# Sums of the hidden-DFT weights kept in DRAM, and seven block products from the second group on

## The chip, the cores and the metric

The kernel runs on one core of one Trainium2 chip. The metric is the time of one execution on the device in microseconds; the time before is 2187.01 us, the median of three runs (2182.2 to 2187.72).

A core has five engines that run side by side and wait for one another through semaphores: PE (TensorE, matrix multiply; PEld is its weight load), DVE (VectorE), ACT (ScalarE), POOL (GpSimd) and SP (SyncE). In this kernel SP issues every DMA, in program order, from one queue. On-chip data lie in SBUF, matmul results in eight PSUM banks, the rest in DRAM.

## The reference

Four layers work on `x` of 2048 rows by 640 columns: attention, Fourier mixing, attention, Fourier mixing. The change concerns the second kind:

```python
a = jnp.einsum("bsd,ed->bse", x, dft_hid_re)
b = jnp.einsum("bsd,ed->bse", x, dft_hid_im)
y = jnp.einsum("ts,bse->bte", dft_seq_re, a) - jnp.einsum("ts,bse->bte", dft_seq_im, b)
x = x + y   # with the layer norm of x as input of a and b
```

Both Fourier layers use the same weights. They are layers 1 and 3 here (layers are counted from 0).

## The kernel before, in words

**Precision.** A float32 operand is cut into a high part (an ACT copy to float32r) and a low part (a subtraction on DVE or POOL), and each product is three matmuls: high by high, high by low, low by high. `split` (L224 to L233) and `cut_part` (L1534 to L1541) do this.

**A Fourier layer** turns the order of the reference round. First come the *sequence passes* (`seq`, L1384): four passes, one for each half of the rows `sb` and part (cosine, sine), each with three stages "a", "b" and "g" of eight units. They multiply the normalized input by the sequence weights `c` and leave the result `u`, transposed, in DRAM (`u_d`). The passes keep a hand-made pipeline: `load_to(n + 3)` issues the loads of `c`, `cut_to(n + 2)` cuts them into a ring of buffers about two units ahead of PE, `x_to` cuts the other operand, and `gather` (L1447) copies or adds up the accumulators at a stage's end. Its stores to `u_d` are put into a list, and `leave` issues them later. The first pass of layer 1 is mixed with the attention before it; that of layer 3 uses sums of `c` which layer 1 kept in DRAM.

Then comes the *column product*: `u` times the 640 x 640 hidden weights `wr`, `wi`. It runs over eight groups `g` of two row tiles (128 rows each). A group by `eight` (L1659) does all eight block products, as two halves of 320 columns for each row tile, with 30 matmuls each: 120 in all. A group by `seven` (L1686) uses a scheme of seven block products with 15 matmuls each, 105 in all, with sums of `u` blocks (`u_s1`, `u_s4`, and `differences` in place) and sums of weight blocks ("t1", "t3", "t4", "t2"). Its order is b11, t1, b21, t2, t3, b22, t4; after each product, adds on DVE and POOL take the bank into the row tiles. The two row tiles of group `g` are `raws[2g]` and `raws[2g + 1]`, each of 640 columns: `x22` is the right half of the second one, and `add(nc.vector, x22, v, x22)` follows t1.

Groups 3, 4, 5 of layer 1 and 3 to 7 of layer 3 are sevens (L1579). Groups 6 and 7 of layer 1 stay eights, with work for the next layer between them.

**The weights' sums.** `load_sums` (L1543 to L1554) loads the ten raw tiles `wr[k]`, `wi[k]` (k = 0 to 4, 128 x 640 each) at the start of the column product, and `make_sums(k)` (L1556 to L1570) makes the four block sums of one k with two adds on POOL, two on DVE, and two splits. They are called between the halves of groups 1 and 2, in both layers, and written to `big2`, `big3` and, for k = 4, two tiles "wt".

**What sets the order around the change.** At the start of the column product SP's queue holds, in this order: three `leave` stores of `u_d`, row tiles 0 and 1, `load_u(1, 1)`, four raw weight tiles, six more stores, `load_u(2, 0)`, row tile 2, six raw weight tiles. Then the group loop begins, with row tile 3 first. `kp1` has room for three `u` loads, the pool "x" for five row tiles. `big2` and `big3` hold the input of the sequence passes until stage "g" of the last pass has cut its last unit. While a seven runs, `coming(g + 1, ...)` makes and cuts the first two operands of the next group.

Of the kernel before, what the change touches and what calls it, by code (L numbers as in the profile page):

```python
# [60 lines left out]
def pairs(c):  # L61
    return [(c[2 * i], c[2 * i + 1]) for i in range(len(c) // 2)]


class Net:
    def __init__(self, nc, tc, ctx, a):
        self.nc, self.tc, self.a = nc, tc, a
        const = ctx.enter_context(tc.tile_pool(name="const", bufs=1))
        self.ln = ctx.enter_context(tc.tile_pool(name="ln", bufs=5))
        self.slots = ctx.enter_context(tc.tile_pool(name="slots", bufs=1))  # L70
        psum = ctx.enter_context(tc.tile_pool(name="psum", bufs=1, space=PSUM))
        self.work = ctx.enter_context(tc.tile_pool(name="work", bufs=2))
# [22 lines left out]
        self.cd = dram.tile([3, NB // 2, P, 512], F32, name="c_d")  # L95
        self.sums_kept = False
# [12 lines left out]
        self.seen = fixed("seen", 2, F32)  # L109
# [1084 lines left out]
    def take_fourier(self):  # L1194
        def halves(t):
            return t.rearrange("p (l c) -> p l c", l=2)

        w = [self.work.tile([P, 2 * D], F32, name="s3", tag="wc") for _ in range(2)]
        self.s3 = sum([cuts(t[:, :1024], 256) for t in w], [])
        self.raws = [t[:, :1024] for t in w + [self.pt[2], self.pt[0], self.pt[1]]]  # L1200
        p = [cuts(t, 512) for t in self.pt]
        self.t1 = p[3] + [self.vq[2]] + self.ou + [p[0][2], p[1][2]]
        half = NB // 2
        first = [("a1", j) for j in range(half)] + [("a2", j) for j in range(half - 1)]
        first += [("b7", 0), ("a2", half - 1), ("b7", 1), ("b5", 0), ("b5", 1)]
        first += [("b", j) for j in range(2, half)] + [("g", j) for j in range(half)]
        self.last_a2 = first.index(("a2", half - 1))
# [176 lines left out]
    def seq(self, n):  # L1384
# [54 lines left out]
        if last and not soon:  # L1439
            self.gather(sb, part, ph)  # L1440

    def leave(self, n=9):
        for f in self.leaving[:n]:
            f()
        del self.leaving[:n]
# [94 lines left out]
        self.nc.vector.tensor_tensor(out=l, in0=src, in1=h.bitcast(F32), op=OP.subtract)  # L1540
        self.made.append((cuts(hi, P), cuts(lo, P)))  # L1541

    def load_sums(self):  # L1543

        c = [self.work.tile([P, 2, 512], F32, name="wt", tag="c", bufs=3).rearrange("p l c -> p (l c)")[:, :D]
             for _ in range(3)]
        self.w_raw = [c[:2], [c[2], self.raw()]]
        for k in range(KC):
            if k == 2:
                yield  # L1550
                self.w_raw += [cuts(t, D) for t in cuts(self.take_qk("kp", 0, F32), 2 * D)]
            for n, t in zip(("wr", "wi"), self.w_raw[k]):
                self.nc.sync.dma_start(t, self.a[n][:, k, :])
        yield  # L1554

    def make_sums(self, k):  # L1556
        nc = self.nc
        if k == 0:
            self.w_sum = sum([pairs(cuts(self.take_big(2 + i), 2 * D)) for i in range(2)], [])
            self.w_sum.append([self.work.tile([P, 2, D], F32R, name="wt", tag="wc").rearrange("p l c -> p (l c)")  # L1560
                               for _ in range(2)])
        r, i = self.w_raw[k]
        (r1, r2), (i1, i2) = cuts(r, 320), cuts(i, 320)
        nc.gpsimd.tensor_tensor(out=r1, in0=r2, in1=r1, op=OP.subtract)
        nc.gpsimd.tensor_tensor(out=r2, in0=r2, in1=i2, op=OP.add)
        nc.vector.tensor_tensor(out=i2, in0=i2, in1=r1, op=OP.add)
        nc.vector.tensor_tensor(out=i1, in0=i2, in1=i1, op=OP.subtract)
        hi, lo = self.w_sum[k]
        for n, t in enumerate((r, i)):
            self.parts_of(hi[:, n * D:(n + 1) * D], lo[:, n * D:(n + 1) * D], t)  # L1570

    def parts_of(self, hi, lo, t):
        self.split(hi, lo, t)

    def fourier(self, xsrc, xdst, more):
        nc = self.nc
        wc = pairs(sum([cuts(t, D) for t in self.big[:2]], []) + cuts(self.qp[0][:, :4 * D], D))
        self.u_raw, self.n_upl = {}, 0
        sevens = range(3, 6 if more else NB // 2)  # L1579
        self.made = deque()  # L1580
        loads = []

# [19 lines left out]
        for n in range(self.un, total):  # L1602
            if n == total - NB:
                weights(range(8))
            if n == total - NB // 2:
                weights(range(8, 10))
                self.take_qk("kp", 1, F32)
            self.seq(n)
            step_w()
            if n >= total - 5 and n < total - 2:  # L1610
                self.load_u((n - total + 5) // 2, (n - total + 5) % 2)
# [27 lines left out]
        def coming(g, n):  # L1639
# [5 lines left out]
                return  # L1645
            a11, a21, a22 = [self.quarter(g, *pz) for pz in ((0, 0), (0, 1), (1, 1))]
            if n == 0:
                add(nc.gpsimd, self.u_s1, a21, a22)
                self.cut_part(a11)
            else:  # L1650
                self.cut_part(self.u_s1)
# [7 lines left out]
        def eight(g, z, sums):  # L1659
            t = 2 * g + z  # L1660
            for n in range(2):
                if z:
# [11 lines left out]
            for hf in range(2):  # L1674
# [4 lines left out]
                add(nc.vector, raws[t][:, cs], p, raws[t][:, cs])  # L1679
                if z and hf:  # L1680
                    differences(g + 1)
                for k in sums[hf]:
                    self.make_sums(k)
            store_x(t)

        def seven(g, halfway):  # L1686
# [5 lines left out]
            def weight(name, k):  # L1692
                if name[0] == "b":
                    k, c = k + KC * (name[1] == "2"), (int(name[2]) - 1) * 320
                    return [w[:, c:c + 320] for w in wc[k]]
                c = ("t1", "t3", "t4", "t2").index(name) * 320
                return [w[:, c:c + 320] for w in self.w_sum[k]]

            def product(p, name, start=True):
                hi, lo = self.made.popleft()  # L1700
# [6 lines left out]
            product(x, "b11")  # L1707
            nc.scalar.activation(p1, x, AF.Copy)
            self.cut_part(a12)
            add(nc.gpsimd, self.u_s4, a12, a11)  # L1710
            product(v, "t1")
            add(nc.vector, x22, v, x22)
            self.cut_part(a11)
# [25 lines left out]
        def before(t):  # L1739
            if not more:  # L1740
                return
            if t == 8:
                self.tmp = cuts(self.kp[0], D)
# [16 lines left out]
        def behind(t):  # L1760
            if more and t >= 12:
# [17 lines left out]
        next(sums)  # L1779
        self.u_sum = [self.slot_tile(n, 512, F32)[:, :320] for n in ("rr1", "rr2", "vq2")]  # L1780
        for g in range(NB // 2):
            load_x(2 * g + 1, 2 * g + 2)
# [4 lines left out]
                seven(g, lambda: before(2 * g + 1) if g < 5 else None)  # L1787
            else:
                for z in range(2):
                    at = 2 * g + z  # L1790
                    eight(g, z, {2: ((), (0,)), 3: ((1,), ()), 4: ((2,), (3,)), 5: ((4,), ())}.get(at, ((), ())))
                    behind(at)
        self.ready, self.hid, self.sums_kept = 8, False, True


# [70 lines left out]
```

## Time and profile before

| what | value |
|---|---|
| median of three runs | 2187.01 us (2182.2 to 2187.72) |
| the profiled execution's own time | 2187.93 us |
| its span, first to last instruction | 2186.2 us |
| granted clock of PE | 0.997 |
| PE / DVE / ACT / POOL busy | 2118.1 / 1603.7 / 1140.5 / 958.0 us |
| moved by DMA | 398.40 MB, mean 182 GB/s |
| later passes of layer 1 (second to fourth) | 678.1 to 973.2 us of the span |
| column product of layer 1 | from 973.17 us |
| column product of layer 3 | from 2051.20 us to the end |

How to read it: the profile is of one execution, and its times are microseconds from the span's start. In a group of instructions stand line, engine, operation, out<-in by the program's names, shapes and count, then busy time, the mean of one in ns, and the idle time before with what ended it. In a timeline stand start, length, engine, line, and in brackets the idle time before with what ended it. In a table of stretches stand start:end, length, the busy time and count of each engine in the order PE, PEld, DVE, ACT, POOL, the granted clock, the share of the 16 DMA engines, and GB/s. "SPq" rows are issues of DMAs, not the transfers.

### The profile page before, as it was taken

The numbers are of one execution on the slowest core, as the hardware profiler recorded it, in microseconds if no ns is written. First come the engines' busy times: TensorE is split into PE (matmuls) and PEld (weight loads), VectorE is DVE, ScalarE is ACT, GpSimd is POOL, SyncE is SP. The second block draws the span as 40 slices with busy tenths as digits, with TensorE's granted clock in tenths as the row PEclk, the third lists the DMA queues.
The fourth block names the chain that finished last, engine by engine and source line by source line (L and its number), as shares of the span: only waits on it lengthen the run. The fifth ranks groups of instructions, "written<-read, shape, count | busy, mean of one in ns | idle before, by whom it ended". The sixth has DMA issues, their size and how long they took to land.

```text
span 2186.2 us, 48927 instructions
## 1 busy us (share of the span) xinstructions
PE 2118.1 (97%) x17872; PEld 1783.2 (82%) x17872; DVE 1603.7 (73%) x3931; ACT 1140.5 (52%) x2125; POOL 958.0 (44%) x1562
## 2 busy tenths in 40 slices
PE   7999999988999999999999999999899999999999
PEld 7987777677878888889999877776778888888899
DVE  6358888886897868786661588888767968677676
ACT  3117777656554545452341177777565645445332
POOL 3037776765614222322430377767655033231324
PEclk9999999999999999999999999999999999999999
DMA  5546666785555354656645556567855454546653
GB/s 183 175 157 190 198 180 215 211 224 169 202 192 189 127 183 141 214 177 207 207 156 167 162 186 200 181 212 226 216 161 182 140 182 132 174 152 208 222 165 125
DMA packets 227089, 398.40 MB, mean 182 GB/s; under 512 B 39969, under 2 KB 86561, under 8 KB 226849
## 3 DMA queue, kind: packets, MB, share of 16 engines
q1 hardware_dynamic: 226848, 395.28, 57.3%
q8 instruction: 141, 2.31, 0.5%
q14 instruction: 100, 0.81, 0.1%
HBM read 273.94 MB, written 120.06 MB: 180 GB/s over the span
## 4 chain that ended last, share of the span: by engine, by line
PE 78%; DVE 7%; DMA 5%; ACT 4%; issue 3%; POOL 2%; SPq 1%; ACTq 0%; DVEq 0%; POOLq 0%
PE banks L1416 29%; PE banks L239 15%; PE banks L257 12%; PE banks L694 6%; PE banks L659 5%; PE banks L1704 5%; PE banks L631 5%; DMA qp<-qk_d 2%; DVE banks L636 1%; ACT pt L669 1%; DMA x_d<-x 1%; PE banks L341 1%; DMA kp<-qk_d 1%; ACT big L1039 1%; DVE qp L232 1%
## 5 line engine op out<-in xcount | busy, mean ns | idle before, releaser
L636 DVE CUSTOM_DVE_ANT_0 banks<-banks,mask 128x384 f32<-128x384 f32 (+2 forms) x1024 | 527.6, 557 | 123.0 <-PE banks L631 99.9
L669 ACT ACTIVATE pt<-banks 128x768 f32<-128x768 f32 (+2 forms) x512 | 393.8, 772 | 168.7 <-PE banks L659 55.2
L675 POOL TENSOR_SCALAR_AFFINE_SELECT pt<-pt 128x256 f32<-128x256 f32 x512 | 213.3, 417 | 213.8 <-ACT pt L669 192.0
L257 PE MATMUL banks<-big,wc 64*128 64x512 f32 x1920 | 271.1, 394 | 0.4 <-DVE pt L442 0.4
L659 PE MATMUL banks<-qp,kp 61*128 61x384 f32 (+2 forms) x1024 | 210.2, 381 | 22.8 <-DVE mc L636 17.4
L694 PE MATMUL banks<-pt,vq 128*32 128x128 f32 x5760 | 211.6, 278 | 3.5 <-ACT pt L669 3.4
L631 PE MATMUL banks<-kp,qp 60*128 60x384 f32 (+2 forms) x1024 | 205.5, 347 | 6.7 <-DVE mc L636 3.1
L257 PEld LDWEIGHTS banks<-big,wc 64*128 64x128 f32 x1920 | 186.8, 185 | 22.6 <-ACT x L544 1.5
L679 POOL TENSOR_SCALAR_AFFINE_SELECT pt<-pt 128x256 f32<-128x256 f32 x448 | 193.8, 433 | 0.0
L226 ACT ACTIVATE qp<-pt 128x512 fp32r<-128x512 f32 (+1 forms) x200 | 123.2, 625 | 128.1 <-DVE pt L1347 51.7
L232 DVE TENSOR_TENSOR qp<-pt,qp 128x512 fp32r<-128x512 f32 (+1 forms) x198 | 156.6, 798 | 42.1 <-ACT qp L226 40.5
L694 PEld LDWEIGHTS banks<-pt,vq 128*32 128x32 f32 x5760 | 142.4, 110 | 51.5 <-issue 35.3
L659 PEld LDWEIGHTS banks<-qp,kp 61*128 61x128 f32 x1024 | 108.0, 184 | 87.3 <-DVE mc L636 65.2
L1416 PE MATMUL banks<-qp,big 128*128 128x512 f32 x648 | 152.9, 390 | 0.0
L631 PEld LDWEIGHTS banks<-kp,qp 60*128 60x128 f32 x1024 | 123.6, 186 | 31.9 <-DVE mc L636 16.4
L1345 POOL TENSOR_TENSOR pt<-pt,pt 128x512 f32<-128x512 f32 x32 | 47.2, 1475 | 231.4 <-DMA pt<-c 173.4
L226 ACT ACTIVATE c<-pt 128x512 fp32r<-128x512 f32 x146 | 90.4, 625 | 111.1 <-POOL pt L1325 57.1
L636 DVE DVE_READ_ACCUMULATOR2_ANT mc<- 128x1 f32 x1024 | 145.0, 142 | 0.0
L1416 PEld LDWEIGHTS banks<-qp,big 128*128 128x128 f32 x648 | 120.8, 188 | 24.2
L232 DVE TENSOR_TENSOR c<-pt,c 128x512 fp32r<-128x512 f32 x144 | 113.8, 793 | 26.9 <-ACT c L226 24.4
L1416 PE MATMUL banks<-qp,xc 128*128 128x512 f32 x480 | 117.4, 391 | 4.3 <-DVE xc L232 2.8
L552 POOL CAST c<-x 128x512 fp32r<-128x512 f32 x64 | 38.9, 611 | 166.5 <-ACT x L544 162.3
(253 smaller groups left out, 4479.9 us busy)
## 6 DMA issues: line engine op xcount, KB each, us to landing
pt<-c SPq DMA_DIRECT2D x166, 512.0 KB
qk_d<-c SPq DMA_DIRECT2D x80, 512.0 KB
kp<-qk_d SPq DMA_DIRECT2D x384, 80.0 KB
qp<-qk_d SPq DMA_DIRECT2D x384, 80.0 KB
kp<-u_d SPq DMA_DIRECT2D x32, 640.0 KB
o_d<-ou SPq DMA_DIRECT2D x64, 256.0 KB
x_d<-x SPq DMA_DIRECT2D x48, 320.0 KB
v_d<-pt SPq DMA_DIRECT2D x16, 768.0 KB
```

The costliest lines, as they stand in the source:

```text
L226: nc.scalar.activation(hi, src, AF.Copy, scale=-1.0 if neg else 1.0)
L232: (eng or nc.vector).tensor_tensor(out=lo, in0=src, in1=hi.bitcast(F32), op=OP.subtract)
L239: self.nc.tensor.matmul(p, x, y, start=n == 0, stop=n == last)
L257: self.nc.tensor.matmul(ps[a], x[r], y[r], start=half + i == 0, stop=half == 1 and i == n - 1, skip_group_check=True)
L631: nc.tensor.matmul(p, qp[quad % 2][b:b + 60, z, qb * P:(qb + 1) * P], kp[quad % 2][b:b + 60, z, k0 * P:(qb + 1) * P], start=True, stop=True)
L636: nc.vector.tensor_tensor_reduce(out=p, in0=p, in1=self.mask[:, 384 - n * P:], scale=1.0, scalar=NEG, op0=OP.add, op1=OP.max, accum_out=mc ...
L659: nc.tensor.matmul(self.banks[:, banks[e], :n * P], kp[quad % 2][b:b + 61, z, kb * P:(kb + 1) * P], qp[quad % 2][b:b + 61, z, kb * P:(kb + ...
L669: nc.scalar.activation(pt[quad, kb][:, 2 * z:2 * z + 2, :n * P], self.banks[:, b0:b1 + 1, :n * P], AF.Exp, scale=SCALE)
L675: nc.gpsimd.affine_select(out=t[:, :, 0:P], in_=t[:, :, 0:P], pattern=[[0, 2], [1, P]], compare_op=OP.is_ge, fill=0.0, base=0, channel_mul ...
L679: nc.gpsimd.affine_select(out=t[:, :, 256:384], in_=t[:, :, 256:384], pattern=[[0, 2], [-1, P]], compare_op=OP.is_gt, fill=0.0, base=0, ch ...
L694: nc.tensor.matmul(self.banks[32 * h:32 * h + 32, bank, :P], vq[:, 96 * (kb % 4) + 21 * h:96 * (kb % 4) + 21 * h + 32], t[:, h, (qb - kb) ...
L1416: nc.tensor.matmul(self.banks[:, bk, :], p, b[q], start=start and m == 0, stop=stop and last and m == 2, skip_group_check=True)
```

## The change

The sums are made once, by a generator `weight_sums(k)`, in stages a and b of the second to fourth pass of layer 1. `weight_step` starts it at unit 1 of stage a (k = 0, 1 in the second pass, 2, 3 in the third, 4 in the fourth) and takes one step of it after each unit: load the two raw tiles; two units later two adds; two more adds; then a split and the stores of its high and low part, twice. All adds are on DVE. The parts are stored in a new DRAM tensor `w_d` of 5 x 4 tiles of 128 x 640.

In both layers `load_sums(k, n)` loads the high and low part of half n (n = 0: t1 and t3; n = 1: t4 and t2) of every k, twenty tiles in all, where ten raw tiles were loaded. The half n = 0 of k = 0 to 3 goes to `big2`, ahead of the first three `leave` stores; n = 1 goes to `big3`, after row tile 2. The calls of `make_sums` go. Sevens begin with group 1. The adds into `u_s1` and `u_s4` go from POOL to DVE. The release of `kp0`, which held the raw tiles of k = 2 to 4, moves to row tile 8.

```diff
+    def weight_sums(self, k):
+        got = [self.raw() for _ in range(2)]
+        for n, t in zip(("wr", "wi"), got):
+            nc.sync.dma_start(t, self.a[n][:, k, :])
+        yield
+        yield
+        (r1, r2), (i1, i2) = [cuts(t, 320) for t in got]
...
+        add(r1, r2, r1, OP.subtract)
+        add(r2, r2, i2)
+        yield
+        add(i2, i2, r1)
+        add(i1, i2, i1, OP.subtract)
+        yield
+        for n, t in enumerate(got):
+            h = self.ln.tile([P, D], F32R, name="x", tag="x")
+            self.split(h, t.bitcast(F32R), t)
+            yield
+            for m, x in enumerate((h.bitcast(F32), t)):
+                nc.sync.dma_start(self.wd[k, 2 * n + m], x)
+        yield
+
+    def weight_step(self, n):
+        if self.sums_kept or n < self.first_len:
+            return
+        sb, part, ph, j = self.order[n]
+        if ph == "a" and j == 1:
+            p = 2 * sb + part - 1
+            self.making = (f for k in ((0, 1), (2, 3), (4,))[p] for f in self.weight_sums(k))
+        if ph != "g":
+            next(self.making, None)
+
+    def load_sums(self, k, n):
+        if k < KC - 1:
+            big = self.big[2 + n]
+            places = [big[:, (2 * k + m) * D:(2 * k + m + 1) * D] for m in range(2)]
+        else:
+            places = cuts(self.work.tile([P, 2 * D], F32R, name="wt", tag="wc"), D)
+        for m, t in enumerate(places):
+            self.nc.sync.dma_start(t.bitcast(F32), self.wd[k, 2 * n + m])
+        self.w_sum[k, n] = places
...
-        sevens = range(3, 6 if more else NB // 2)
+        sevens = range(1, 6 if more else NB // 2)
...
             self.seq(n)
+            self.weight_step(n)
...
-                add(nc.gpsimd, self.u_s1, a21, a22)
+                add(nc.vector, self.u_s1, a21, a22)
...
-                for k in sums[hf]:
-                    self.make_sums(k)
...
-            add(nc.gpsimd, self.u_s4, a12, a11)
+            add(nc.vector, self.u_s4, a12, a11)
...
+        load_x(0, 1)
+        self.take_big(2)
+        for k in range(KC - 1):
+            self.load_sums(k, 0)
         self.leave(3)
-        load_x(0, 1)
         self.load_u(1, 1)
-        sums = self.load_sums()
-        next(sums)
+        self.load_sums(KC - 1, 0)
         self.leave()
         self.load_u(2, 0)
         load_x(2)
-        next(sums)
+        self.take_big(3)
+        for k in range(KC):
+            self.load_sums(k, 1)
```

More of the change, by code (lines that the diff above doesn't have):

```diff
@@ L95, in __init__ @@
         self.cd = dram.tile([3, NB // 2, P, 512], F32, name="c_d")
+        self.wd = dram.tile([KC, 4, P, D], F32, name="w_d")
         self.sums_kept = False
@@ L1206, in take_fourier @@
         first += [("b", j) for j in range(2, half)] + [("g", j) for j in range(half)]
+        self.first_len, self.making = len(first), iter(())
         self.last_a2 = first.index(("a2", half - 1))
@@ L1440, in seq, with add @@
             self.gather(sb, part, ph)
+    def weight_sums(self, k):
+        nc = self.nc
+        got = [self.raw() for _ in range(2)]
[4 more added lines that the diff above has]
+        (r1, r2), (i1, i2) = [cuts(t, 320) for t in got]
+        def add(out, a, b, op=OP.add):
+            nc.vector.tensor_tensor(out=out, in0=a, in1=b, op=op)
+        add(r1, r2, r1, OP.subtract)
[29 more added lines that the diff above has]
+        self.w_sum[k, n] = places
     def leave(self, n=9):
@@ L1541, in cut_part @@
         self.made.append((cuts(hi, P), cuts(lo, P)))
[L1543 to L1573, printed above, removed]
     def fourier(self, xsrc, xdst, more):
@@ L1578, in fourier @@
         self.u_raw, self.n_upl = {}, 0
-        sevens = range(3, 6 if more else NB // 2)
+        sevens = range(1, 6 if more else NB // 2)
+        self.w_sum = {}
         self.made = deque()
@@ L1657, in differences, with eight @@
                 add(nc.vector, a11, a11, self.u_s1, OP.subtract)
-        def eight(g, z, sums):
+        def eight(g, z):
             t = 2 * g + z
@@ L1695, in weight @@
                     return [w[:, c:c + 320] for w in wc[k]]
-                c = ("t1", "t3", "t4", "t2").index(name) * 320
-                return [w[:, c:c + 320] for w in self.w_sum[k]]
+                n, c = divmod(("t1", "t3", "t4", "t2").index(name), 2)
+                return [w[:, c * 320:c * 320 + 320] for w in self.w_sum[k, n]]
             def product(p, name, start=True):
@@ L1742, in before @@
             if t == 8:
-                self.tmp = cuts(self.kp[0], D)
+                self.tmp = cuts(self.take_qk("kp", 0, F32), D)
                 self.home = [self.home[i] for i in (2, 3, 0, 1)]
@@ L1789, in fourier @@
                 for z in range(2):
-                    at = 2 * g + z
-                    eight(g, z, {2: ((), (0,)), 3: ((1,), ()), 4: ((2,), (3,)), 5: ((4,), ())}.get(at, ((), ())))
-                    behind(at)
+                    eight(g, z)
+                    behind(2 * g + z)
         self.ready, self.hid, self.sums_kept = 8, False, True
```

## The prediction

> **What bounds the kernel now.** I read the page first: busy shares and the chain of work that ended last.
>
> ```profile
> span 2186.2 us, 48927 instructions
> PE 2118.1 (97%) x17872; PEld 1783.2 (82%) x17872; DVE 1603.7 (73%) x3931; ACT 1140.5 (52%) x2125; POOL 958.0 (44%) x1562
> PE 78%; DVE 7%; DMA 5%; ACT 4%; issue 3%; POOL 2%; SPq 1%; ACTq 0%; DVEq 0%; POOLq 0%
> ```
>
> PE is busy 97% of the span and carries 78% of the chain. So in the stages that change, time is matmul count plus the places where PE waits. Next the stage table (columns: start:end, length, then busy time and instruction count of PE, PEld, DVE, ACT, POOL, clock, DMA share, GB/s), with stretches cut at the group borders that the PE timeline shows. First layer 1's column product, groups 0, 1, 3, 4, 5; then layer 3's groups 0, 3 and 4.
>
> ```profile
> 973.20:990.80 17.60, 17.60 (x122) 17.60 (x121) 7.60 (x9) 2.74 (x4) 9.45 (x8) 1.00 0.92 315
> 990.80:1008.40 17.60, 17.60 (x122) 17.60 (x122) 6.91 (x11) 2.23 (x4) 4.17 (x4) 1.00 0.85 276
> 1026.00:1042.60 16.60, 15.66 (x107) 15.40 (x107) 12.17 (x16) 5.02 (x9) 7.28 (x5) 1.00 0.43 128
> 1042.60:1058.00 15.40, 15.40 (x107) 15.40 (x107) 11.04 (x15) 5.17 (x9) 7.87 (x5) 1.00 0.77 269
> 1058.00:1075.10 17.10, 15.62 (x107) 15.36 (x105) 11.10 (x16) 6.67 (x11) 5.75 (x4) 1.00 0.62 198
> ...
> 2051.20:2068.80 17.60, 17.60 (x122) 17.60 (x121) 7.42 (x9) 2.74 (x4) 9.49 (x8) 1.00 0.98 324
> 2104.00:2120.60 16.60, 15.66 (x108) 15.40 (x107) 12.20 (x16) 5.03 (x9) 7.27 (x5) 1.00 0.39 125
> 2120.60:2136.00 15.40, 15.40 (x108) 15.40 (x107) 11.03 (x15) 5.17 (x9) 7.46 (x5) 1.00 0.53 172
> ```
>
> A group of eight products takes 17.60 us with PE busy throughout; a settled group of seven takes 15.40. The first seven of each layer takes 16.60, and layer 1's last one (group 5) 17.10. Why those two are longer decides what the change meets, so their rows:
>
> ```profile
> 1029.46 2.24 DVE L1540 TENSOR_TENSOR pt<-kp,pt 128x640 fp32r<-128x640 f32 x1
> 1029.44 1.57 POOL L1637 TENSOR_TENSOR pt<-kp 128x640 f32<-128x640 f32 x1 [4.76 <-DVE kp L1637]
> 1031.75 1.29 PE L1704 MATMUL banks<-big,pt 128*128 128x320 f32 x7 [0.94 <-DVE pt L1540]
> 1046.10 0.82 DVE L1540 TENSOR_TENSOR pt<-kp,pt 128x640 fp32r<-128x640 f32 x1
> 1062.05 1.11 SPq L1631 DMA_DIRECT2D x<-x_d  x2
> 1065.21 0.49 DVE L1637 TENSOR_TENSOR x<-banks,x 128x320 f32<-128x320 f32 x1 [2.89 <-DMA x<-x_d]
> 1066.49 1.73 PE L1704 MATMUL banks<-big,pt 128*128 128x320 f32 x10 [1.48 <-DVE pt L1540]
> ```
>
> In the first seven, the subtraction of `cut_part(a12)` takes 2.24 us instead of 0.82, because POOL's `u_s4` add (1.57) runs beside it, and PE waits. In group 5, DVE's add into `x22` waits for the load of that row tile (issued 1062.05, used 1065.21: 3.2 us). Behind the add in DVE's queue stands `cut_part(a11)`, which the fourth product (`t2`) needs; PE goes on at 1066.49, which is 1.28 us after the add starts. Keep this second chain in mind: row tile lands, add, cut, `t2`.
>
> **Multiplies.** Groups 1 and 2 of both layers go from eight to seven: 4 x (17.60 - 15.40) = **-8.8 us**. The `u_s4` and `u_s1` adds leave POOL for DVE, where such an operation costs 0.82. Then the first seven has no POOL add beside the cut: 2 x (16.60 - 15.40) = **-2.4**. Group 5's 1.7 stays, since its load is not moved. A settled seven gets 2 x 0.82 more on a DVE busy 11.04 of 15.40; about 12.7 still fits, so nothing.
>
> **Sums no longer made in the column product.** Per layer POOL loses ten adds, DVE ten adds and ten subtractions, ACT ten copies. PE is busy 17.60 of 17.60 where they ran, so this gives nothing.
>
> **Sums made in layer 1's passes.** Five times four adds and two subtractions on DVE, two copies on ACT:
>
> ```profile
> 1000.17 0.48 DVE L1566 TENSOR_TENSOR wt<-wt 128x320 f32<-128x320 f32 x1
> L226 ACT ACTIVATE big<-kp 128x640 fp32r<-128x640 f32 x8 | 5.7, 733 | 9.2 <-DVE kp L1567 9.2
> 678.10:710.80 32.70, 32.70 (x146) 27.06 (x146) 18.97 (x23) 11.79 (x21) 13.84 (x9) 1.00 0.66 215
> 710.80:738.00 27.20, 27.20 (x122) 22.53 (x121) 23.01 (x36) 15.18 (x32) 4.95 (x4) 1.00 0.42 135
> 906.80:934.00 27.20, 27.20 (x121) 22.53 (x121) 25.93 (x41) 16.97 (x35) 4.87 (x3) 1.00 0.62 205
> 934.00:973.20 39.20, 38.21 (x167) 30.80 (x167) 35.58 (x51) 25.77 (x48) 8.40 (x6) 1.00 0.47 151
> ```
>
> DVE: 5 x (4 x 0.48 + 2 x 0.82) = 17.8 us; ACT 10 x 0.73 = 7.3. Two sets go into each of the second and third passes, one into the fourth. In stage a DVE is idle 13.7 of 32.7; in stage b 4.2 of 27.2, and a set is 3.6. So it fits, tightly in b. The nearest row for what overfull costs is the last pass, where weight cuts bring DVE to 25.93 of 27.20 in b and 35.58 of 39.20 in g; there PE loses 39.20 - 38.21 = 1.0 us. Bounds: nothing, to all 17.8 on PE. I take 0.6, near the first. Thirty DMAs of 0.33 MB join SP's queue there: 9.8 MB into stages whose DMA share is 0.42 to 0.66. A store waits on SP for DVE's cut; behind it stands the next load of `c`, whose cut runs about two units ahead of PE, so I cost that at nothing. Without that lead, each such wait would be some 0.8 us on PE.
>
> **Loading the sums: the disputed term.** Before, ten raw tiles were loaded and needed from group 3 on. Now twenty tiles of 0.328 MB are loaded and needed in group 1. What counts is SP's queue, in order: row tiles 0 and 1; eight tiles of n=0 (once `big2` is free); three stores of `u_d`; `u` of group 1; the last two n=0 tiles; six stores; `u` of group 2; row tile 2; the ten n=1 tiles; and only then **row tile 3**, which is the `x22` of group 1. That is group 5's chain again, in both layers.
>
> ```profile
> 966.52 0.42 DVE L232 TENSOR_TENSOR vq<-big,vq 128x256 fp32r<-128x256 f32 x1
> 961.00:967.00 6.00, 6.00 (x28) 4.99 (x27) 5.64 (x11) 4.83 (x10) 0.00 (x0) 1.00 0.00 0
> 2044.48 0.42 DVE L232 TENSOR_TENSOR vq<-big,vq 128x256 fp32r<-128x256 f32 x1
> 4.40:17.40 13.00, 7.31 (x26) 6.00 (x27) 11.36 (x30) 4.66 (x9) 8.39 (x8) 1.00 0.93 347
> 972.00:998.00 26.00, 26.00 (x176) 25.77 (x175) 11.93 (x15) 2.74 (x4) 14.67 (x12) 1.00 0.94 318
> 2050.00:2076.00 26.00, 26.00 (x176) 25.77 (x176) 11.76 (x15) 2.74 (x4) 15.05 (x12) 1.00 0.98 325
> 980.00:985.00 5.00, 5.00 (x36) 5.00 (x35) 2.84 (x3) 2.58 (x4) 2.84 (x3) 1.00 1.04 404
> u_d<-kp SPq DMA_DIRECT2D x48, 256.0 KB
> kp<-u_d SPq DMA_DIRECT2D x32, 640.0 KB
> x<-x_d SPq DMA_DIRECT2D x36, 320.0 KB
> ```
>
> `big2` is last read by a cut that ends at 966.9, and the queues stand idle from 961 to 967, so the stream starts at 967.0. It holds 8 + 2 + 10 sum tiles and two row tiles (22 x 0.328 = 7.21 MB), nine stores (2.36) and two `u` loads (1.31): 10.88 MB. The first tile takes 3.2 us (as in group 5), the other 10.55 MB go at the stream's rate. Rows for that: 318 and 325 GB/s where queues were full in this very place with stores and `u` loads mixed in, 347 at the kernel's start, where nearly all are plain loads like these, and 404 at best. Two thirds of the bytes here are plain loads: I take **347**. Row tile 3 is usable at 967.0 + 3.2 + 10.55 / 0.347 = 1000.6. Group 1 starts at T = 990.8; `t2` starts after three products of 15.40 / 7 = 2.2, and its third matmul, at T + 6.9, needs the cut that is ready 1.28 after the tile. So the stall is 1000.6 + 1.28 - 997.7 = 4.2 us. Layer 3 is the same schedule (free at 2044.9, group 1 at 2068.8: both 1078.0 later). Together **+8.4**. The n=1 tiles themselves land before row tile 3, within this stall. Bounds: by 404, 996.3 and no stall; by 318, 1003.4 and 7.0 each; by the 276 of group 1's own stretch, 1008.4 and 12.0 each.
>
> The Trainium skill, page "DMA: Bandwidth & Descriptors", section "Bandwidth", gives 341 GB/s for a 1 MB transfer and 425 for 16 MB; by the second, an estimate from that page, row tile 3 would be there in time and the stall gone. The rows agree with the first figure; only 5 us here come near the second.
>
> **Sum.** -8.8 - 2.4 + 0.6 + 8.4 = -2.2 us. The profiled execution took 2187.93 us, 1.73 more than its span; it lies 0.92 above the median of 2187.01. On the median: 2187.01 - 2.2 = **2184.8 us**. About 0.3% (6.6 us) is what a measurement of this kernel can tell from no change.
>
> **Rivals.** *Full-rate stream.* At 404 GB/s no first seven waits: -11.2 + 0.6 gives 2176.4. For it: POOL makes no sums beside the stream. Against: 404 held in one 5 us stretch, 318 to 325 over 26.
>
> *Slow stream, slower than before.* One mechanism: row tile 3 behind twenty sum tiles, DVE held by `x22`, PE by `t2`. The gain is used up when each stall reaches 5.3, that is a tile later than 1001.7 or a rate under 335. By 318: -11.2 + 0.6 + 14.0 = +3.4, 2190.4; by 276: +13.4, 2200.4. For it: both rows in this place are under 335. Against: a third of their bytes are stores and `u` loads.
>
> *Passes on the path.* If stage b's cover of 4.2 us is not there when needed, half of the 17.8 shows: +8.9 on the sum, 2193.7. Against: PE there is busy 27.20 of 27.20, with DVE ahead.
>
> *DVE held by `u`.* The `u_s1` add now stands in DVE's order ahead of the next group's cut.
>
> ```profile
> 2144.07 4.79 SPq L1528 DMA_DIRECT2D kp<-u_d  x2
> 2147.60 2.29 DVE L1540 TENSOR_TENSOR qp<-kp,qp 128x640 fp32r<-128x640 f32 x2
> 2149.16 2.16 POOL L1637 TENSOR_TENSOR pt<-kp 128x640 f32<-128x640 f32 x1
> ```
>
> Its load goes out at 2144.07; POOL's add started at 2149.16 without a wait (group start 2136.0 + 13.2). DVE would reach it at about +12.4. Add and cut (1.64) must be done by +15.4, so PE loses only from a landing after about +13.8. One us later than that in ten sevens is +10, 2194.8.
>
> **How the numbers follow.** Forecast case (each stall 1 to 7 us): 0.58. Full rate: 0.20. Slow stream beyond 7: 0.10. Passes: 0.06. DVE held: 0.06. Faster by over 0.3% needs both stalls and the passes under 4.6 us together: all of the full-rate case and 0.06 of the forecast case, 0.26. Slower by over 0.3% needs over 17.8: most of the last three, 0.15. Within: 0.59. Range: from no stall (2176) to stalls of 9 each with 1.5 in the passes (2187.0 - 11.2 + 18 + 1.5 = 2195): the slower half of the slow stream stays out.
>
> **What would show it.** Right: seven-product groups of 15.40 from the second seven on; in group 1 a PE row at `t2` that waits for the cut, with DVE's `x22` add just before it waiting for `x<-x_d`; passes of layer 1 with PE full. Wrong: PE full through group 1 (stream faster), PE waiting for `big<-w_d` at `t1` (n=0 late), idle PE in the passes' stage b, or PE waits at `b11` behind the `u_s1` add.

## The result and the profile after

The changed kernel took 2191.81 us, the median of 14 runs (2187.53 to 2196.02). The kernel before, run beside it, took 2184.07 us (14 runs, 2176.97 to 2194.82). The ratio is 1.0031, with a 95% interval from 1.0016 to 1.0045: by that ratio 6.8 us slower, where 2.2 us faster was predicted. The same kernel was measured twice more beside the kernel before in the experiments below, with ratios of 1.0009 [0.9996, 1.0021] and 1.0002 [0.9988, 1.0017]. Its own medians in the three sets of runs were 2191.81, 2191.96 and 2189.76 us; those of the kernel before were 2184.07, 2189.31 and 2190.16 us. So it was the kernel before that came out low in the first set. Taken together, the change costs between nothing and a few us: what was predicted as a small gain is a small loss or nothing.

First two lines from the head of the page of the changed kernel:

```profile
span 2190.1 us, 48868 instructions
...
PE 2113.7 (97%) x17812; PEld 1779.6 (81%) x17812; DVE 1622.1 (74%) x3973; ACT 1141.0 (52%) x2131; POOL 920.4 (42%) x1538
```

PE has 60 matmuls fewer but only 4.4 us less busy time (2118.1 before), where 8.8 us were to go. So PE does not only wait more: it is also slower somewhere. The table of stretches, cut at the group borders, shows where. The columns are those of the prediction's table. Here are, of layer 1, group 0, group 1, 3.4 us inside group 1, and groups 2 and 5; then, of layer 3, the same groups 0 and 1, the stretch inside group 1, and group 2:

```profile
976.50:994.09 17.59, 17.59 (x121) 17.59 (x120) 7.50 (x10) 0.74 (x1) 4.96 (x4) 1.00 1.04 368
994.09:1015.18 21.09, 17.20 (x107) 16.93 (x106) 11.39 (x17) 5.05 (x8) 3.56 (x3) 0.92 0.70 251
1005.80:1009.20 3.40, 3.40 (x15) 3.40 (x14) 1.26 (x3) 0.00 (x0) 0.32 (x1) 0.51 0.70 228
1015.18:1030.58 15.40, 15.40 (x107) 15.40 (x106) 11.60 (x18) 5.06 (x8) 3.57 (x3) 1.00 0.53 172
...
1061.38:1077.99 16.61, 15.67 (x108) 15.41 (x106) 11.25 (x17) 6.32 (x10) 3.58 (x3) 1.00 0.65 211
2054.73:2072.33 17.60, 17.60 (x122) 17.60 (x121) 7.50 (x10) 0.74 (x1) 4.96 (x4) 1.00 1.05 358
2072.33:2093.63 21.30, 17.19 (x107) 16.93 (x106) 11.39 (x17) 5.06 (x8) 3.56 (x3) 0.92 0.72 262
2084.50:2087.90 3.40, 3.40 (x14) 3.40 (x14) 1.30 (x3) 0.00 (x0) 0.70 (x1) 0.50 0.71 226
2093.63:2109.03 15.40, 15.40 (x107) 15.40 (x106) 11.60 (x18) 5.06 (x8) 3.58 (x3) 1.00 0.53 171
```

From group 2 on, a seven takes 15.40 us with PE full, as forecast. Group 1 takes 21.09 and 21.30 us in place of 15.40. Of the 5.69 us too much in layer 1, 3.89 are PE idle (21.09 - 17.20), and 1.80 are PE busy for longer with the same 105 matmuls. The clock column says why: over the group it is 0.92, and for 3.4 us behind the wait it is a half. Group 5, which waits 0.94 us and keeps its clock, is busy for 15.67, so a wait by itself adds 0.27; the other 1.5 us are what 3.4 us of half clock cost. Matmul by matmul, in the PE timeline of the changed kernel (layer 1, then layer 3):

```profile
1000.69 0.46 PE L1723 MATMUL banks<-big,pt 128*128 128x320 f32 x2
1005.04 2.38 PE L1723 MATMUL banks<-big,pt 128*128 128x320 f32 x10 [3.89 <-DVE pt L1591]
1007.22 1.01 PE L1723 MATMUL banks<-wt,pt 128*128 128x320 f32 x3
1008.02 2.49 PE L1723 MATMUL banks<-big,pt 128*128 128x320 f32 x12
1010.34 0.60 PE L1723 MATMUL banks<-wt,pt 128*128 128x320 f32 x3
...
2083.49 2.24 PE L1723 MATMUL banks<-big,pt 128*128 128x320 f32 x10 [4.11 <-DVE pt L1591]
```

Two matmuls of `t2` go, and the third waits for DVE's cut, as forecast. Then the ten left of `t2` with `big`, its three with `wt`, and the first twelve of `t3` take 2.38, 1.01 and 2.49 us; at full clock three of them take 0.60, as in the fifth row. On DVE the chain is the one that the prediction asked the reader to keep in mind:

```profile
998.34 0.82 DVE L1658 TENSOR_TENSOR pt<-kp 128x640 f32<-128x640 f32 x1
1003.76 0.49 DVE L1658 TENSOR_TENSOR x<-banks,x 128x320 f32<-128x320 f32 x1 [4.61 <-issue]
1004.17 0.81 DVE L1591 TENSOR_TENSOR pt<-kp,pt 128x640 fp32r<-128x640 f32 x1
```

DVE does the `u_s4` add at 998.34, then stands 4.61 us at the add into `x22`. The cut for `t2` stands behind it and starts at 1004.17; PE goes on at 1005.04. The profile names no releaser for the 4.61 us ("issue"); that it was row tile 3 is read from SP's timeline, where its load goes out only at 997.24, behind the n=1 tiles, and is shown by the experiments `e2_row3_first` and `e6_x22_late`:

```profile
997.24 0.32 SPq L1652 DMA_DIRECT2D x<-x_d  x1
```

### The profile page after: what moved, and what is told of

The parts are those of the page before. It is cut to its first block, busy times and chain, and to the rows that moved or that the text cites. A ratio compares the mean times of both kernels' runs of the same rounds, so it can differ in the third digit from the quotient of the medians.

```text
span 2190.1 us, 48868 instructions
## 1 busy us (share of the span) xinstructions
PE 2113.7 (97%) x17812; PEld 1779.6 (81%) x17812; DVE 1622.1 (74%) x3973; ACT 1141.0 (52%) x2131; POOL 920.4 (42%) x1538
## 4 chain that ended last, share of the span: by engine, by line
PE 78%; DVE 7%; DMA 5%; ACT 3%; issue 3%; POOL 3%; SPq 1%; ACTq 0%; DVEq 0%; POOLq 0%
PE banks L1418 29%; PE banks L240 12%; PE banks L258 12%; PE banks L1723 8%; PE banks L695 6%; PE banks L660 5%; PE banks L632 4%; DVE banks L637 1%; DMA kp<-qk_d 1%; DMA qp<-qk_d 1%; ACT pt L670 1%; DVE qp L233 1%; PE banks L342 1%; DMA rr<-r_d 1%; ACT big L1040 1%
## 5 line engine op out<-in xcount | busy, mean ns | idle before, releaser
L1418 PEld LDWEIGHTS banks<-qp,xc 128*128 128x128 f32 x480 | 89.6, 188 | 25.1 <-DVE xc L233 5.0
```

The source lines that it names most:

```text
L1418: nc.tensor.matmul(self.banks[:, bk, :], p, b[q], start=start and m == 0, stop=stop and last and m == 2, skip_group_check=True)
```

## The experiments

**The theory** after the first result: row tile 3, behind the ten n=1 tiles on SP, holds DVE at `x22` and so PE at `t2`, and each wait is made dearer by half clock. **Rivals**: the new DRAM tensor shifts where data lie; making the sums in the passes costs time; the n=1 tiles themselves are late; the slow matmuls behind the wait come from the transfers of that moment, not from the wait.

### The place of the new tensor: `e1_placed`

```diff
 # in before
+        self.wd = dram.tile([KC, 4, P, D], F32, name="w_d")
```

> The kernel before with the new DRAM tensor w_d allocated and never used; nothing else differs. Three theories of the change's 6.8 us. Theory 'stall': all of it comes from the column products, so this kernel takes the time of the kernel before, within 3 us. Rival 'place': w_d moves the tensors behind it in DRAM and slows the attention layers, where the profile after is 3.6 us behind by 527 us of the span, long before any changed instruction: then this kernel is 3.5 to 7 us slower. Rival 'passes': making the sums in layer 1's passes costs it: then nothing here.

Measured: 2186.85 us (12 runs) beside 2189.21 (23 runs), ratio 0.999 [0.9977, 1.0003]. The tensor's place costs nothing that can be told.

### Row tile 3 first: `e2_row3_first`

```diff
-        load_x(2)
+        load_x(2, 3)
         self.take_big(3)
```

> The changed kernel, with row tile 3 loaded right after row tile 2, ahead of the ten n=1 tiles. Theory 'stall': the two stalls of 3.9 and 4.1 us at t2, and the 3.4 us at half clock behind each (1.7 us lost), were row tile 3's. The last n=1 tile now lands 0.8 us later, about 1003.7 in the profile's time, and t2 needs it at 1002.5, so a wait of some 1.2 us for wt stays in each layer, too short for a half clock: 2 x (5.7 - 1.2) = 9 us faster than the changed kernel, about 2 us faster than the kernel before or, if part of the 6.8 us is noise, up to 9 faster. If DVE's add into x22 was not what held PE (rival 'tiles': PE waits for the n=1 tiles anyway), the stall stays at 4 to 5 us and the time that of the changed kernel.

Measured: 2180.82 us (5 runs), ratio to the kernel before 0.9964 [0.9952, 0.9976]. One load moved ahead by ten places turns the change into a gain. In layer 1's PE timeline, `t2` goes through its first twelve matmuls without a wait; only the three with `wt` take 0.95 us where 0.60 is usual:

```profile
995.68 1.92 PE L1723 MATMUL banks<-big,pt 128*128 128x320 f32 x12
997.44 0.95 PE L1723 MATMUL banks<-wt,pt 128*128 128x320 f32 x3
```

In layer 3 PE waits 0.38 us there, for the last sum tile. The 1.2 us expected for that tile in each layer did not come, so it lands earlier than was reckoned.

### Making the sums alone: `e3_making`

The kernel before, with `weight_sums` run in the passes and its results stored; nothing reads them, and the column product is the old one.

```diff
 # in before
+        self.wd = dram.tile([KC, 4, P, D], F32, name="w_d")
+        self.first_len, self.making = len(first), iter(())
...
             self.seq(n)
+            self.weight_step(n)
```

> The kernel before with w_d and with the making of the sums in layer 1's later passes (loads, adds, splits, stores to w_d), but the column products as before: their sums are made again there and w_d is not read. Theory 'stall': PE stays full in the passes, so 0 to 1 us slower than the kernel before. Rival 'passes': 4 to 9 us slower, with PE idle in the second to fourth pass of layer 1. Rival 'place': as slow as the kernel with w_d alone.

Measured: 2188.97 us (11 runs), ratio 0.9999 [0.9989, 1.0009]. The passes take the work at no cost that can be told. The profile of the changed kernel shows it too, in the table of stretches for stages a and b of the second pass and stage g of the fourth:

```profile
681.50:714.20 32.70, 32.70 (x146) 27.10 (x145) 22.00 (x29) 13.21 (x23) 13.89 (x9) 1.00 0.80 267
714.20:741.40 27.20, 27.20 (x122) 22.53 (x121) 25.71 (x42) 15.43 (x32) 4.09 (x3) 1.00 0.61 216
...
937.40:976.50 39.10, 38.08 (x167) 30.63 (x165) 35.56 (x51) 25.70 (x48) 8.41 (x6) 1.00 0.58 186
```

DVE's busy time in stage b rose from 23.01 to 25.71 of 27.20, and PE stayed full. The last stage is as it was (39.10 now, 39.20 before).

### Stores and `u` behind the sums: `e4_order`

```diff
-        self.leave()
-        self.load_u(2, 0)
-        load_x(2)
+        load_x(2, 3)
         self.take_big(3)
         for k in range(KC):
             self.load_sums(k, 1)
+        self.load_u(2, 0)
+        self.leave()
```

> The changed kernel with another order at the start of the column product: row tiles 2 and 3 and the ten n=1 tiles come ahead of the load of u for group 2 and of the last six stores of u_d. Six stores (4.7 us between landings in the profile after) and one u load (2.6 us) no longer stand ahead of the n=1 tiles, so the last of these lands about 996.4 in the profile's time, six us before t2 needs it. Theory 'stall': no wait at t2 in either layer, no half clock, so 11.4 us faster than the changed kernel and 4 to 11 us faster than the kernel before. Rival 'place' or 'passes': 11.4 us faster than the changed kernel too, but never more than some 5 us faster than the kernel before, since their cost stays.

Measured: 2182.1 us (5 runs), ratio 0.997 [0.9958, 0.9982]. It can't be told from `e2_row3_first`. `t2` no longer waits in either layer. What is left on PE is a wait at the start of group 2, in layer 1 of 0.60 us (in layer 3 0.97):

```profile
1007.49 2.75 PE L1723 MATMUL banks<-big,qp 128*128 128x320 f32 x17 [0.60 <-DVE qp L1591]
```

DVE's timeline names its source:

```profile
1005.88 0.82 DVE L1658 TENSOR_TENSOR pt<-kp 128x640 f32<-128x640 f32 x1 [2.36 <-DMA kp<-u_d]
```

That is the `u_s1` add, now on DVE, waiting 2.36 us for the second load of `u` of group 2. It is the rival "DVE held by `u`" of the prediction, at one group in place of ten sevens. None of the three traces of the changed kernel has it, and all of the versions without the larger wait but `e8_best` do: 0.26 and 1.27 us in `e2_row3_first`, 0.90 and 1.30 in `e6_x22_late`.

### The changed kernel again: `e5_after_again` and `e10_after_third`

> The changed kernel as it is, once more. If the trace's account is whole (column products about as long as before: 11.2 us saved by the two groups and given back by two waits of 4.0 us with 1.7 us of half clock each, which is 11.4), it is within 0 to +3.5 us of the kernel before. If something outside the two column products costs as well, it is again +5 us or more, and the place is found where this profile and the first agree against before. In the profile: PE waits of about 4 us at the t2 product of group 1 in both layers, and the granted clock at a half for 3.4 us right behind each.

> The changed kernel as it is, beside the filled one. By the two traces of it so far the two column products come to -0.1 and +1.8 us against the kernel before: within -1 and +4 us of before in time. If the first comparison (+6.8 us) is the true one, +5 us or more.

Measured: 2191.96 us (12 runs) beside 2189.31 (28 runs), ratio 1.0009 [0.9996, 1.0021]; and 2189.76 us (11 runs) beside 2190.16 (23 runs), ratio 1.0002 [0.9988, 1.0017]. Both are within the bounds given for the trace's account, and neither bears out +5 us. PE waited 4.82 and 4.43 us at `t2` in the one, 4.49 and 4.59 in the other, with half clock at each. The longest wait, in the PE timeline of `e5_after_again`, and after it one of `e10_after_third`:

```profile
1003.22 3.03 PE L1723 MATMUL banks<-big,pt 128*128 128x320 f32 x10 [4.82 <-DVE pt L1591]
```

```profile
2083.05 3.03 PE L1723 MATMUL banks<-big,pt 128*128 128x320 f32 x10 [4.59 <-DVE pt L1591]
```

Ten matmuls take 3.03 us there, where they took 2.38 and 2.24 in the first trace: the half clock set in before the wait was over. In these two places it lasts 6.8 us, at the other four waits of the three traces 3.4.

### DVE freed instead of the load moved: `e6_x22_late`

```diff
-            add(nc.vector, x22, v, x22)
             self.cut_part(a11)
             product(x, "b21", start=False)
             add(nc.vector, x11, x, x11)
             self.cut_part(a21)
+            add(nc.vector, x22, v, x22)
```

> The changed kernel with the addition into x22 put behind the cut of t2's operand on DVE; no transfer is moved. If t2 waits because DVE stands at x22 for row tile 3, the 4 us waits go, t2 waits at most 0.5 us for the last n=1 sum tile, no half clock follows, and the time falls by 10 to 11.5 us against the changed kernel: 7 to 8 us below before in the same runs. If t2 waits for the n=1 sum tiles themselves (they land too late on the queue), the wait stays at 3 to 4 us and the time with it.

Measured: 2184.9 us (11 runs), ratio to the kernel before 0.9968 [0.9953, 0.9984], 7.1 us below the changed kernel in the same set of runs. No transfer was moved, row tile 3 still comes last, and yet the 4 us waits are gone. What is left in layer 1's PE timeline is small, a wait in `t2` and the one at the start of group 2:

```profile
997.73 0.56 PE L1723 MATMUL banks<-wt,pt 128*128 128x320 f32 x2 [0.21 <-DMA wt<-w_d]
...
1006.08 2.18 PE L1723 MATMUL banks<-big,qp 128*128 128x320 f32 x13 [0.90 <-DVE qp L1591]
```

The gain is less than the 10 to 11.5 us expected against the changed kernel; against the kernel before, the 7 to 8 us expected lie within the interval. The two column products of its trace take 223.95 us, 10.1 less than the mean of 234.0 in the three traces of the changed kernel. So the n=1 tiles were in time but for 0.21 us (0.34 in layer 3); what cost the time was that an add which nobody needs yet stood in DVE's queue ahead of a cut that PE needs.

### How long a wait must be: `e7_position`

Row tile 3 behind eight of the ten n=1 tiles in layer 1, behind nine in layer 3.

```diff
+            if more and k == KC - 1:
+                load_x(3)
-            self.load_sums(k, 1)
+            self.load_sums(k, 1, None if more or k < KC - 1 else lambda: load_x(3))
```

> The changed kernel with the load of row tile 3 put behind eight of the ten n=1 tiles in layer 1 and behind nine of them in layer 3; its place in the queue sets how long t2 waits. By 0.82 us for each tile that it passes: waits of about 2.3 us in layer 1 and 3.1 us in layer 3, instead of 3.9 and 4.1. If half clock follows every wait of PE above about 1.5 us, both layers show 3.4 us at 0.500 behind the wait. If it needs a wait of more than about 3 us (a whole stretch of 3.4 us nearly idle), layer 1 shows none, and layer 3 may or may not. Against the changed kernel: 2.4 us less by the waits alone, 4 to 6 us less where half clock goes too.

Measured: 2186.66 us (10 runs), ratio 0.9991 [0.9974, 1.0007]; 5.3 us below the changed kernel. The PE timeline shows both waits, and in layer 3 slow matmuls behind it:

```profile
997.93 1.73 PE L1725 MATMUL banks<-big,pt 128*128 128x320 f32 x10 [2.46 <-DVE pt L1593]
...
2073.26 1.79 PE L1725 MATMUL banks<-big,pt 128*128 128x320 f32 x10 [3.28 <-DVE pt L1593]
2074.84 1.00 PE L1725 MATMUL banks<-wt,pt 128*128 128x320 f32 x3
```

The waits are 2.46 and 3.28 us (2.3 and 3.1 were expected): one place in the queue is worth about 0.8 us. Half clock followed the longer one only. All the drops of the clock in one trace lie a whole number of steps of 3.41 us apart, so the stretches are cut on that grid:

```profile
996.20:999.60 3.40, 1.67 (x11) 1.67 (x12) 2.36 (x4) 0.00 (x0) 0.00 (x0) 1.00 0.70 278
2071.40:2074.80 3.40, 1.54 (x10) 1.54 (x11) 2.36 (x4) 0.00 (x0) 0.00 (x0) 1.00 0.58 209
2074.80:2078.20 3.40, 3.40 (x15) 3.40 (x14) 1.22 (x2) 0.00 (x0) 1.69 (x2) 0.50 0.76 252
```

PE was idle for 1.73 us of the first stretch, and the clock held; it was idle for 1.86 us of the second, and the third ran at half. One pair is no threshold, but a wait shorter than a step was enough. Over all twelve traces, from 25 us of the span on, every one of the 18 steps at full clock in which PE was idle for 1.85 us or more was followed by half clock, 30 of the 95 with 1.3 to 1.85 us were, and of the others, thousands, one was. The Trainium skill, page "TensorE: Matmul & The Clock Gate", section "Part 1: The HAM clock gate", puts the half clock behind at least one idle window of about 3.4 us, on a free-running grid of 3413 ns. The traces agree with the grid, the length and the half; where the sentence is read as a window that is idle throughout, they don't: PE worked 1.54 us of that step.

### The wait filled with work: `e9_filler`

```diff
+            if g == 1:
+                for _ in range(22):
+                    nc.tensor.matmul(z, wc[0][0][:, :P], wc[0][0][:, :320], start=True, stop=True,
+                                     skip_group_check=True)
             product(y, "t2")
```

> The changed kernel with 22 more 128x128 by 128x320 matmuls in group 1 between the products b21 and t2, whose result is overwritten by t3's and read by nothing; they fill some 3.5 us of the 3.9 to 4.8 us for which PE otherwise stands. Row tile 3, x22 and t2's operand come no earlier, so t2 starts no earlier. If the half clock is set off by PE's standing still, none follows t2's start in either layer, and the time falls by 1.7 to 2.7 us for each layer, 3.4 to 4.4 us in all, against the changed kernel. If the slow matmuls behind the wait have another cause (the transfers of that moment, or the tiles that have just been written), the granted clock still falls to a half there, or the first 25 matmuls of t2 and t3 still take half as long again, and the time is that of the changed kernel or more.

Measured: 2188.76 us (12 runs), ratio to the kernel before 1.0005 [0.9989, 1.0022], 1.0 us below `e10_after_third`; the intervals are too wide to tell that from the 3.4 to 4.4 us expected. The PE timeline of layer 1 answers what the times can't:

```profile
1002.89 3.39 PE L1740 MATMUL banks<-big 128*128 128x320 f32 x22
1006.11 0.46 PE L1723 MATMUL banks<-big,pt 128*128 128x320 f32 x2
1007.60 1.73 PE L1723 MATMUL banks<-big,pt 128*128 128x320 f32 x10 [1.04 <-DVE pt L1591]
1009.17 0.60 PE L1723 MATMUL banks<-wt,pt 128*128 128x320 f32 x3
1009.61 1.92 PE L1723 MATMUL banks<-big,pt 128*128 128x320 f32 x12
```

The row tile comes no sooner and the transfers are the same, but behind a wait of 1.04 us the ten, three and twelve matmuls take 1.73, 0.60 and 1.92 us instead of 2.38, 1.01 and 2.49. In layer 3 the wait is 1.23 us, and the granted clock stays at 1.00 in both. The half clock comes from PE standing still, not from the transfers.

### The best order: `e8_best`

`e4_order`, and in sevens the load of the next odd row tile, which waits on SP for a store to land, moved behind the load of `u`:

```diff
-            if not more or g < 4:
-                load_x(2 * g + 3)
+            ahead = [2 * g + 3] if not more or g < 4 else []
+            if g not in sevens:
+                load_x(*ahead)
             if g in sevens:
                 before(2 * g)
-                seven(g, lambda: before(2 * g + 1) if g < 5 else None)
+                seven(g, lambda: (load_x(*ahead), before(2 * g + 1) if g < 5 else None))
```

> The order of e4 (row tiles 2 and 3 ahead of the n=1 tiles, the second load of u and the six stores behind them), and in the seven-product groups the load of the next odd row tile moved behind the load of u, so that u(2,1) no longer waits on SP for the landing of row tile 0's store. Expected: u(2,1) lands some 2 us earlier, the DVE addition for u_s1 no longer waits for it, and PE's waits of 0.60 us (layer 1) and 0.97 us (layer 3) at the start of group 2 go: 1 to 2 us below e4, 8 to 12 us below before. If those waits have another cause (the DMA's own time, or DVE's work behind it), they stay and the time is that of e4.

Measured: 2174.37 us (6 runs, 2173.69 to 2181.3), ratio to the kernel before 0.9935 [0.9916, 0.9955]: 14.2 us faster, the lowest of all versions. That is more than the 8 to 12 us expected, and its median lies 7.7 us below that of `e4_order`, from another set, where 1 to 2 were expected; by the column products of the two traces (221.15 and 223.37 us) the difference is 2.2. In the trace of `e4_order` SP waited 3.2 us for the store of a row tile. DVE's `u_s1` add here waits 0.82 us instead of 2.36, and PE no longer waits for it:

```profile
1001.71 0.83 DVE L1658 TENSOR_TENSOR pt<-kp 128x640 f32<-128x640 f32 x1 [0.82 <-DMA kp<-u_d]
```

## Why the prediction was wrong

**The account.** Here the whole column product is one stretch, from its first matmul to the first of group 6 in layer 1, and to the end of the last product in layer 3. The second number is the length, the third PE's busy time, the third from the end the clock. The kernel before:

```profile
973.17:1075.10 101.93, 99.52 (x677) 98.99 (x675) 65.16 (x90) 29.41 (x45) 39.31 (x29) 1.00 0.67 223
2051.20:2182.35 131.15, 130.22 (x886) 129.69 (x884) 85.64 (x118) 37.53 (x57) 54.75 (x39) 1.00 0.55 180
```

The changed kernel:

```profile
976.50:1077.99 101.49, 96.66 (x647) 96.13 (x645) 64.66 (x94) 27.30 (x43) 22.86 (x19) 0.98 0.71 242
2054.73:2186.19 131.46, 127.35 (x856) 126.82 (x854) 86.12 (x126) 34.80 (x55) 30.00 (x25) 0.99 0.57 195
```

`e5_after_again`:

```profile
973.75:1076.81 103.06, 97.58 (x647) 97.05 (x645) 64.56 (x94) 27.25 (x43) 22.89 (x19) 0.97 0.71 237
2054.73:2186.52 131.79, 127.36 (x856) 126.83 (x854) 86.04 (x126) 34.73 (x55) 29.98 (x25) 0.99 0.57 193
```

`e10_after_third`:

```profile
972.00:1074.02 102.02, 96.64 (x646) 96.12 (x645) 64.61 (x94) 27.24 (x43) 22.93 (x19) 0.98 0.71 240
2053.81:2186.09 132.28, 127.69 (x856) 127.16 (x854) 86.21 (x126) 34.72 (x55) 30.10 (x25) 0.97 0.57 192
```

`e9_filler`:

```profile
978.69:1078.71 100.02, 98.35 (x669) 97.82 (x668) 64.68 (x94) 27.25 (x43) 22.89 (x19) 1.00 0.72 246
2055.81:2186.08 130.27, 129.04 (x878) 128.51 (x876) 85.51 (x126) 34.73 (x55) 29.99 (x25) 1.00 0.58 196
```

`e8_best`:

```profile
970.80:1066.40 95.60, 94.86 (x647) 94.59 (x645) 64.02 (x94) 27.24 (x43) 22.98 (x19) 1.00 0.75 257
2042.52:2168.07 125.55, 125.55 (x856) 125.29 (x854) 85.42 (x126) 34.72 (x55) 30.12 (x25) 1.00 0.60 203
```

Both layers together: before 233.08 us; changed kernel 232.95, 234.85 and 234.30, mean 234.0; filled 230.29; best order 221.15. With no wait left but 0.74 us in group 5, the seven products save 233.08 - 221.15 = 11.9 us. The waits and what follows them cost 234.0 - 221.15 = 12.9 us. The column products of `e1_placed` and `e3_making`, which run the old code, took 231.2 and 230.9 us in their traces, so the trace of before was about 2 us long, and the saving is 10 to 12. By the traces the change comes to +0.9 us against that of before and +2.3 against the mean of the three; the three ratios say +6.8, +2.0 and +0.4.

Point by point, by the prediction's steps:

- **Multiplies, -8.8: right.** Group 2 takes 15.40 us in both layers of the changed kernel, and so does group 1 in `e8_best`. **The first seven, -2.4: right for the trace used, and luck in part.** The wait of 0.94 us that it goes by is in neither `e1_placed` nor `e3_making`. There POOL's `u_s4` add starts a moment after DVE's cut and not before it, and the cut keeps its 0.82 us (`e1_placed`; first DVE's timeline, then POOL's); its first seven takes 15.79 us, not 16.60. Both terms, and what group 5 waits less, are 11.9 us against the trace of before and 10 to 12 against all three.

```profile
1029.73 0.82 DVE L1541 TENSOR_TENSOR pt<-kp,pt 128x640 fp32r<-128x640 f32 x1
1029.89 2.09 POOL L1638 TENSOR_TENSOR pt<-kp 128x640 f32<-128x640 f32 x1 [4.75 <-DVE kp L1638]
```

- **Group 5's 1.7, said to stay: 1.2** (16.61 us) in the first trace.
- **Sums made in the passes, +0.6: nothing that can be told**, by `e3_making`.
- **The stream at 347 GB/s: right.** Row tile 3 was forecast 33.6 us behind the first load. The first load goes out at 970.39, and DVE uses the tile at 1003.76, 33.4 us later. The stretch between them in the trace of the changed kernel, with 352 GB/s in its last column:

```profile
970.39:1003.68 33.29, 30.76 (x195) 29.44 (x193) 15.87 (x21) 9.09 (x15) 5.97 (x4) 1.00 0.98 352
```

- **Where row tile 3 stops the work: right.** `e6_x22_late` shows that it is DVE's order that passes the wait on, and `e2_row3_first` that it is SP's order that makes it.
- **The two waits, 4.2 each: right as waits, wrong as the price.** The three traces show 3.89, 4.11, 4.82, 4.43, 4.49 and 4.59, mean 4.4. **This term, +8.4, is the step that failed**: it priced a wait of PE at its length. At each of the six stood 3.4 us or more of half clock, and the two layers cost 12.9 us instead of 8.4. Of the missing 4.5 us, 0.4 are the length of the waits (8.8 us in two layers), 0.5 the 0.27 us that a wait adds by itself, and 3.6 are left for the half clock. They turn -2.2 into about +2. `e9_filler` takes the half clock away and leaves the row tile where it was: its column products are 4.0 us below those of `e10_after_third`. The trace of before had half clock to be seen in three places, at 422.3 us in the attention of layer 0, and at 599.8 and 1685.2 in the first passes of layers 1 and 3, the last two right behind waits of PE of 1.05 us; the prediction read the clock only as a mean of 1.00 in the stages that change.
- **The rivals.** Full-rate stream: no. Slow stream, slower: its mechanism is the one that happened, but not for its reason; the gain was used up at a wait of 4.4 us, where the prediction put that point at 5.3, because the half clock adds its share. Passes on the path: no. DVE held by `u`: not in the changed kernel, and 0.26 to 1.30 us a layer in the versions named under `e4_order`.

**What stays open.** Why the first result gave +6.8 us is not shown; the kernel before was 5 to 6 us lower in it than in the three other sets of its runs (2189.21 to 2190.16), and the changed kernel was not higher. The profiled execution of the changed kernel is 3.9 us longer than that of before, with column products of equal length; most of the rest arises in the attention of layer 0, ahead of any changed instruction. In the same way `e8_best` is 17.6 us below `e5_after_again` in time, where their column products differ by 13.7.

The traces show one thing that such differences go with: half clock in stages that the change does not touch. Outside the column products the granted clock is a half for 13.7 us in the trace of before, for 17.1 in the first one of the changed kernel and in `e5_after_again`, for 20.5 in `e9_filler` and 6.8 in `e8_best`. The time outside the column products is 1953.1, 1957.2, 1955.6, 1959.7 and 1950.8 us, in the same order. At some 1.5 us for each 3.4 (an estimate, from group 1 above), this comes to 4.5 us of the 4.7 between `e5_after_again` and `e8_best`, but to 1.5 us only of the 4.1 between before and the changed kernel. It also hides what `e9_filler` gains: its span is that of `e10_after_third`, 2190.0 us. So part of the 14.2 us of `e8_best` may be chance; its column products alone are 10 to 12 us shorter than those of the old code. The same kernel has such stretches in one execution and not in the next (3.4 us more in two traces of the changed kernel than in the third), and why is not shown.

## What to carry to other kernels

When a change lets the work start sooner, go down the queues again: a tile that was loaded in time as the last of a group may now be the first one that is missing, and an operation that nobody needs yet can stand on its engine ahead of one that TensorE needs. Price a wait of TensorE of 3.3 us and more at its length plus about half of the half-clock stretch that comes with it, here 4.4 us plus about 2. One load moved ahead of ten others, or one addition moved behind two cuts, brought about as much here (11.1 and 7.1 us against the changed kernel, the first across two sets of runs) as the 60 matmuls that the change removes (8.8).

## What the runs showed of the hardware that was not expected

- The granted clock falls to a half for one or two steps of 3.41 us when TensorE has waited, and the fall can come before the wait is over. All seven waits at `t2` of 3.28 us and more had it; that of 2.46 us, and those of 1.5 us and less in the column products, had none. What counts is more the idle time within one step than the length of a wait: at 1.85 us and more in a step, half clock followed every time (18 of 18); at 1.3 to 1.85 in 30 of 95; below that once.
- TensorE's matmuls don't have to be useful to hold the clock: 22 whose result nobody reads were enough.
